# Attention and a routed mixture of experts on one core: the rows of q, k and v loaded in shorter pieces

## Chip, cores and metric

The kernel runs on 1 core of one Trainium2 chip. The metric is the device time of one execution in microseconds. Before the change it is 684.65 us in the median of 3 runs (682.07 to 686.68).

## What is computed

The reference is a causal attention, half of whose heads look at the last 32 positions and half at every 32nd position, followed by a mixture of experts with two levels of routing. Shapes are those of q, k and v: 8 batches, 8 heads, 576 positions, 64 columns, all in float32; 16 experts in 4 groups, of size 512 x 1024 and 1024 x 512.

```python
scores = scale * np.matmul(q, k.transpose(0, 1, 3, 2))          # scale = 1 / 8
rel = pos[:, None] - pos[None, :]
mask_local = (rel >= 0) & (rel < 32)                            # heads 0 to 3
mask_strided = (rel >= 0) & (pos[None, :] % 32 == pos[:, None] % 32)   # heads 4 to 7
attn = softmax(np.where(masks, scores, -1e9)); x = np.matmul(attn, v)
# x as 4608 tokens of 512 columns
g_idx = np.argmax(x @ w_group, axis=1)                          # group, with its softmax weight g_w
e_idx = np.argmax(xg @ w_expert[g], axis=1)                     # expert in it, with weight e_w
out[token] = g_w * e_w * (np.maximum(x[token] @ w1[g, e], 0) @ w2[g, e])
```

## The kernel before

**Layout.** The host rearranges q, k and v into four DRAM tensors: `sq` (q and k of the strided heads, transposed), `ll` (q and k of the local heads, transposed), `vs` and `vl` (v of both, each head with a column of ones). Each has 128 rows a batch, one for each partition. A row is cut into three pieces, one for each group of units: 864, 864 and 648 floats for `sq`, 1024, 1024 and 256 for `ll`, 520, 520 and 390 for `vs`, 520, 520 and 130 for `vl`. In DRAM the pieces of a row start at `SO`, `LO` and `VO`, multiples of 64 floats, and the pitch of a row is a multiple of 64 floats as well. One DMA moves one piece of all 128 rows: one contiguous run a row, up to 4096 bytes.

**Attention.** A batch has five units (`DOUBLES`): two of the strided heads ("s"), two of the local ones ("l") and one of both ("m"). `step(s)` issues the work of four units at once, by hand and in a fixed order on every engine: the QK matmuls of unit s into PSUM (L243, L248), Exp of unit s-1, mask, maximum and subtraction of unit s (DVE L256 and L259, POOL L260), the PV matmuls and the normalization of unit s-2 (L284, L290 to L292), and for unit s-3 the store of x to DRAM (`store_x`, L304 to L313) and its transposes for the routing. POOL copies shifted rows of v (L941, L942).

**Loads.** All loads and stores of this stage are issued by SP, in program order, on one hardware queue. `load_qk` and `load_v` (L916 to L933) load a unit's pieces. Those of the first batch are issued ahead of the loop, with the constants behind the first of them. From then on step g of batch b issues two loads of batch b + 1, behind the stores of that step (`pieces`, L969). Two sets of buffers alternate (`bufs[b % 2]`), so a piece is loaded about one batch before it is read. The first half of expert 0's W1 is loaded within the last batch (L579).

**Instructions.** The attention is written out without loops: the matmuls and weight loads of TensorE in this stage are some 8,700 instructions in a row. Their code comes from DRAM too, in packets of a queue of its own (q8 of the profile) on the same 16 DMA engines.

**Experts.** Behind the attention, tokens are gathered for each expert by indirect DMAs, and two matmuls in three products of split float32 follow (L633, L685). The weights come in pieces of 512 KB: the first weight in rows of 4 KB, the second in rows of two runs of 2 KB (L561).

Of the kernel before, what the change touches and what calls it, by code (L numbers as in the profile page):

```python
# [19 lines left out]
B, H, S, D = 8, 8, 576, 64  # L20
# [26 lines left out]
SW = [8 * 4 * UN // 2, 8 * 4 * UN // 2, 4 * 3 * UN]  # L47
SO = [0, 896, 1792]
SPITCH = 2496
LW = [1024, 1024, 256]  # L50
LO = [0, 1024, 2048]
LPAD = 32
LTILE = LPAD + sum(LW)
VW = 2 * (D + 1)
SVW = [4 * VW, 4 * VW, 3 * VW]
VO = [0, 576, 1152]
SVPITCH = 1600
LVW = [4 * VW, 4 * VW, VW]
LVPITCH = 1344
# [13 lines left out]
CW = SEL0 + G + NE  # L73


def unit_rows(u):

    return min(RES, STRIDE - RES * u)


def unit_order():

    return [t * STRIDE + RES * u + r for u in range(NU) for t in range(TR) for r in range(unit_rows(u))]


def host_arrays(q, k, v, moe_w_group, moe_w_expert, moe_w1, moe_w2):
    f = np.float32
    qT = np.ascontiguousarray(np.asarray(q, f).transpose(0, 1, 3, 2))
    kT = np.ascontiguousarray(np.asarray(k, f).transpose(0, 1, 3, 2))

    byhead = lambda x: x.reshape(B, 2, 2, D, S).transpose(0, 2, 3, 1, 4).reshape(B, 128, 2, S)
    bytoken = lambda x: x.reshape(B, 2, 2, S, D).transpose(0, 2, 3, 1, 4)
    sq = np.zeros((B, 128, SPITCH), f)
    order = unit_order()
    rmaj = lambda x: np.pad(byhead(x[:, 4:])[..., order], ((0, 0), (0, 0), (0, 0), (0, NU * UN - S)))
    both = np.stack([rmaj(qT), rmaj(kT)], axis=2)
    for g in range(3):
        x = both[:, :, :, :, 4 * UN * g:min(4 * g + 4, NU) * UN].reshape(B, 128, -1)
        sq[:, :, SO[g]:SO[g] + SW[g]] = x

    ql = byhead(qT[:, :4])
    kl = byhead(kT[:, :4]).reshape(B, 128, 2, S // 64, 2, 32)[:, :, :, :, ::-1].reshape(B, 128, 2, S)
    both = np.stack([ql, kl], axis=2)
    ll = np.concatenate([both[:, :, :, :, 256 * g:256 * g + 256].reshape(B, 128, -1) for g in range(3)], axis=2)

    v = np.asarray(v, f)
    vs = np.zeros((B, 2, GAP, SVPITCH), f)
    x = np.zeros((B, 2, NU * UN, 2, D + 1), f)
    x[:, :, :S, :, :D] = bytoken(v[:, 4:])[:, :, order]
    x[..., D] = 1.0  # L110
    x = x.reshape(B, 2, NU, UN, VW).swapaxes(2, 3)
    vl = np.zeros((B, 128, LVPITCH), f)
    y = np.ones((B, 2, S, 2, D + 1), f)
    y[..., :D] = bytoken(v[:, :4])
    y = y.reshape(B, 2, S // 64, 2, 32, VW)[:, :, :, ::-1].reshape(B, 2, S // 64, 64, VW)
    y = y.swapaxes(2, 3).reshape(B, 128, S // 64, VW)
    for g in range(3):
        vs[:, :, :UN, VO[g]:VO[g] + SVW[g]] = x[:, :, :, 4 * g:4 * g + 4].reshape(B, 2, UN, -1)
        vl[:, :, VO[g]:VO[g] + LVW[g]] = y[:, :, 4 * g:4 * g + 4].reshape(B, 128, -1)
    wr = np.concatenate([moe_w_group] + [moe_w_expert[g] for g in range(G)], axis=1)  # L120
    wr = np.pad(wr.reshape(4, 128, G + NE).transpose(1, 0, 2), ((0, 0), (0, 0), (0, 32 - G - NE)))

    cst = np.zeros((128, CW), f)
    p = np.arange(128)[:, None]
    w = np.arange(GAP)[None, :]
    i = p % GAP
    for o, m in ((0, RES), (3 * GAP, unit_rows(NU - 1))):
        ok = (w < m * TR) & (i < m * TR) & (w % m == i % m) & (w // m <= i // m)
        cst[:, o:o + GAP] = np.where(ok, 0.0, MASKED)
    key = np.where(p // LB % 2 == 0, w - LB, np.where(w < LB, w, w - 2 * LB))  # L130
    ok = (key <= p % LB) & (key > p % LB - STRIDE)
    cst[:, GAP:2 * GAP] = np.where(ok, 0.0, MASKED)
    cst[:, 2 * GAP:3 * GAP] = np.where(ok & ((key >= 0) | (p >= LB)), 0.0, MASKED)
    cst[:, IOTA0:TRI0] = np.arange(128)
    cst[:, TRI0:SML0] = np.arange(96)[None, :] > p
    sm = cst[:, SML0:WR0]
    cst[:, WR0:SEL0] = wr.reshape(128, -1)
    cst[:, SEL0:] = p % 32 == np.arange(G + NE)
    sm[:, 0:16] = np.arange(16) * (EST // TB)
    sm[:, 16:20] = [4, 3, 2, 1]  # L140
    sm[:, 20:21] = p
    sm[:, 64:64 + NSL] = (EST // 128 * np.arange(NE)[:, None] + np.arange(NB)).reshape(1, -1)
    sm[:, 24:24 + len(NVAR) - 1] = NVAR[:-1]
    sm[:, 48:48 + NTOK // CAP] = CAP * np.arange(1, NTOK // CAP + 1)
    return {
        "sq": sq, "ll": np.ascontiguousarray(ll), "vs": vs.reshape(B, 128, SVPITCH), "vl": vl, "cst": cst,
        "w1": np.ascontiguousarray(moe_w1.reshape(NE, DM, FF)),
        "w2": np.ascontiguousarray(moe_w2.reshape(NE, FF, DM)),
    }
# [148 lines left out]
def store_x(tc, k, b, xd, x, g):  # L298

    nc = tc.nc  # L300
    xb = xd[b * S:(b + 1) * S, :]
    kind, n = DOUBLES[g]
    if kind == "l":
        nc.sync.dma_start(xb[n * 256:(n + 1) * 256, 0:256].rearrange("(u p) c -> p u c", p=128),  # L304
                          x.rearrange("p (u c) -> p u c", c=256))
        return
    xs = xb[:, 256:512].rearrange("(t r) c -> t r c", r=STRIDE)
    for kind, u, a, p in rows_of(g):
        if kind == "s":
            m = unit_rows(u)  # L310
            nc.sync.dma_start(xs[:, RES * u:RES * u + m], x[p:p + m * TR, a * 256:(a + 1) * 256])
    if DOUBLES[g][0] == "m":
        nc.sync.dma_start(xb[512:576, 0:256], x[64:128, 256:512])  # L313
# [490 lines left out]
def build_all(nc, d, out):  # L804
    k = Ctx()
    with tile.TileContext(nc, schedule_with_timeline_sim=True) as tc, ExitStack() as top:
# [86 lines left out]
        with ExitStack() as ms:  # L893
# [6 lines left out]
            for i in range(2):  # L900
                p = early[i].enter_context(pool(f"early{i}", side="right" if i else "left"))
# [7 lines left out]
            def clear(i):  # L909
                _, ll, _, _, even = bufs[i]  # L910
                nc.gpsimd.memset(ll[:, 0:LPAD], 0.0)
                nc.gpsimd.memset(even[:, 0:VW], 0.0)

            clear(0)

            def load_qk(b, g):  # L916
                kind, n = DOUBLES[g]
                sq, ll = bufs[b % 2][:2]
                if kind != "l":
                    nc.sync.dma_start(sq[n], d["sq"][b, :, SO[n]:SO[n] + SW[n]])  # L920
                if kind != "s":
                    nc.sync.dma_start(ll[:, LPAD + LO[n]:LPAD + LO[n] + LW[n]],
                                      d["ll"][b, :, LO[n]:LO[n] + LW[n]])

            def load_v(b, g):
                kind, n = DOUBLES[g]
                _, _, vs, vl, vl2 = bufs[b % 2]
                if kind != "l":
                    nc.sync.dma_start(vs[:, 4 * VW * n:4 * VW * n + SVW[n]],
                                      d["vs"][b, :, VO[n]:VO[n] + SVW[n]])  # L930
                if kind != "s":
                    x, y = 4 * VW * n, 4 * VW * n + LVW[n]
                    nc.sync.dma_start(vl[:, x:y], d["vl"][b, :, VO[n]:VO[n] + LVW[n]])  # L933

            def shift_v(b, g, h):
                n = DOUBLES[g][1]
# [7 lines left out]
            def step(s):  # L944
# [16 lines left out]
                if u:  # L961
                    for g, h in shifts[u.g] if s > 1 else (((1, 0), (1, 64)) if s else ()):
                        shift_v(u.b, g, h)
                    for f in ahead.get(u.g, ()):
                        if u.b + 1 < B:
                            f(u.b + 1)
                run_due()

            pieces = {0: [(load_qk, 0), (load_qk, 1)], 1: [(load_qk, 2), (load_v, 0)],  # L969
                      2: [(load_qk, 3), (load_v, 1)], 3: [(load_qk, 4), (load_v, 2)],  # L970
                      4: [(load_v, 3), (load_v, 4)]}
            ahead = {g: [lambda b, f=f, h=h: f(b, h) for f, h in fs] for g, fs in pieces.items()}
            shifts = [[(1, 0)], [(1, 64)], [(4, 0)], [(4, 64)], [(3, 0), (3, 64)]]
            units = []
            fixed, k.fixed = ExitStack(), True
            fixed.enter_context(tc.manual_schedule())
            load_qk(0, 0)
            load_consts(tc, k, cp, lp, d["cst"])
            load_qk(0, 1)
# [11 lines left out]
            for b in range(B):  # L991
# [5 lines left out]
                for g in range(len(DOUBLES)):  # L997
                    u = Ctx()
# [24 lines left out]
    return k  # L1023


_SHAPES = {"sq": (B, 128, SPITCH), "ll": (B, 128, sum(LW)), "vs": (B, 128, SVPITCH),
           "vl": (B, 128, LVPITCH), "cst": (128, CW),
           "w1": (NE, DM, FF), "w2": (NE, FF, DM)}


def make_program():
    import concourse.bacc as bacc

    nc = bacc.Bacc("TRN2", target_bir_lowering=False, num_devices=1)
    d = {n: nc.dram_tensor(n, s, F32, kind="ExternalInput").ap() for n, s in _SHAPES.items()}
    out = nc.dram_tensor("out", (NTOK, DM), F32, kind="ExternalOutput").ap()
    build_all(nc, d, out)
    return nc
# [8 lines left out]
```

## Time and profile before

| What | Value |
|---|---|
| Median of 3 runs | 684.65 us |
| The profiled execution's own time | 686.05 us |
| Its span in the profile | 684.3 us |
| TensorE busy in the span | 620.5 us (91%) |
| VectorE, ScalarE, GpSimd busy | 394.3, 352.0, 257.7 us |
| DMA packets | 64,120, 127.82 MB |
| Mean granted TensorE clock | 0.966 of full speed |

The profile is of one execution; its span is a little shorter than the time that the device reports. In the slices each digit is a fortieth of the span (17.1 us) in tenths of it; the attention fills about the first eleven. PE is TensorE's matmul, PEld its weight load, DVE VectorE, ACT ScalarE, POOL GpSimd, SP the engine that issues the DMAs; an engine with a q behind it is its sequencer. In a row of waits stand the engine that waited, its line, what ended the wait, the total, the count and the longest; "issue" is time in which the engine waited for nothing that the profile shows. A row of the DMA queues has packets, MB and the time that the packets took as a share of 16 engines over the stretch. A packet is what one engine moves as one piece; each DMA adds a packet of 4 bytes on each of its engines, which are among those under 512 B.

### The profile page before, as it was taken

The numbers are of one execution on the slowest core, as the hardware profiler recorded it, in microseconds if no ns is written. First come the engines' busy times: TensorE is split into PE (matmuls) and PEld (weight loads), VectorE is DVE, ScalarE is ACT, GpSimd is POOL, SyncE is SP. The second block draws the span as 40 slices with busy tenths as digits, with TensorE's granted clock in tenths as the row PEclk, the third lists the DMA queues.
The fourth block names the chain that finished last, engine by engine and source line by source line (L and its number), as shares of the span: only waits on it lengthen the run. The fifth ranks groups of instructions, "written<-read, shape, count | busy, mean of one in ns | idle before, by whom it ended". The sixth has DMA issues, their size and how long they took to land.

```text
span 684.3 us, 17927 instructions
## 1 busy us (share of the span) xinstructions
PE 620.5 (91%) x7140; PEld 530.8 (78%) x7141; DVE 394.3 (58%) x640; ACT 352.0 (51%) x621; POOL 257.7 (38%) x336
## 2 busy tenths in 40 slices
PE   5788778778788999999999999999999999999991
PEld 4666566556547798989989889889898898989981
DVE  6557667667755745575475555774655556455120
ACT  2455536454614645575475555764645557455220
POOL 6558665566623522251332422532324223220110
PEclk9999999999879999999999999999999999999996
DMA  9888876786516663573744936755548465362100
GB/s 334 261 271 248 248 214 188 223 266 196 142 37 203 218 233 126 198 239 131 269 158 149 286 119 236 244 182 198 196 130 274 133 233 184 137 208 82 36 18 23
DMA packets 64120, 127.82 MB, mean 187 GB/s; under 512 B 12640, under 2 KB 24928, under 8 KB 63976
## 3 DMA queue, kind: packets, MB, share of 16 engines
q1 hardware_dynamic: 56296, 106.78, 49.0%
q0 software_dynamic: 7680, 18.91, 7.4%
q8 instruction: 116, 1.90, 1.1%
q14 instruction: 28, 0.23, 0.1%
HBM read 109.91 MB, written 22.04 MB: 193 GB/s over the span
## 4 chain that ended last, share of the span: by engine, by line
PE 66%; issue 3%; DVE 2%; ACT 1%; DMA 1%; POOL 1%; POOLq 0%; DVEq 0%; ACTq 0%
PE pair L633 21%; PE bank L685 16%; PE pair L685 12%; PE bank L633 7%; PE bank L693 4%; PE pair L606 2%; PE pair L847 1%; DMA raw<-w 1%; PE pair L358 1%; DVE wL L565 1%; PE bank L373 0%; POOL out L669 0%; DVE xL L614 0%; ACT wH L564 0%; PE pair L284 0%
## 5 line engine op out<-in xcount | busy, mean ns | idle before, releaser
L565 DVE TENSOR_TENSOR wL<-raw,wH 128x1024 fp32r<-128x1024 f32 x122 | 146.1, 1230 | 29.5 <-ACT wH L564 21.4
L564 ACT CAST wH<-raw 128x1024 fp32r<-128x1024 f32 x124 | 125.7, 1063 | 19.4 <-DMA raw<-w 11.5
L633 PE MATMUL pair<-xH,wH 128*128 128x248 f32 (+10 forms) x384 | 114.0, 297 | 0.6 <-PE bank L847 0.6
L633 PE MATMUL pair<-xL,wH 128*128 128x248 f32 (+10 forms) x384 | 114.1, 297 | 0.0
L633 PE MATMUL pair<-xH,wL 128*128 128x248 f32 (+10 forms) x384 | 114.0, 297 | 0.0
L669 POOL DMA_INDIRECT out<-y,idx x48 | 56.1, 1168 | 143.3 <-ACT y L664 97.7
L652 DVE SCALAR_TENSOR_TENSOR hL<-pair,hH 128x384 fp32r<-128x384 f32 x96 | 53.2, 556 | 86.4 <-ACT hH L651 86.3
L651 ACT ACTIVATE hH<-pair 128x384 fp32r<-128x384 f32 x96 | 47.0, 491 | 96.5 <-PE pair L633 47.9
L633 PEld LDWEIGHTS pair<-xH,wH 128*128 128x128 f32 x384 | 72.3, 188 | 1.8 <-issue 1.1
L633 PEld LDWEIGHTS pair<-xL,wH 128*128 128x128 f32 x384 | 72.3, 188 | 0.6
L633 PEld LDWEIGHTS pair<-xH,wL 128*128 128x128 f32 x384 | 72.2, 188 | 0.0
L656 POOL CAST hX<-hH 128x512 fp32r<-128x512 f32 x16 | 9.8, 611 | 162.8 <-issue 150.2
L594 POOL DMA_INDIRECT xg<-xd,idx x48 | 58.1, 1210 | 18.2 <-issue 14.3
L685 PE MATMUL bank<-wH,hH 128*128 128x512 f32 x160 | 63.4, 396 | 0.0
L685 PE MATMUL bank<-wL,hH 128*128 128x512 f32 x160 | 63.4, 396 | 0.0
L685 PE MATMUL bank<-wH,hL 128*128 128x512 f32 x160 | 63.1, 394 | 0.0
L260 POOL TENSOR_TENSOR pr<-pr,mx 128x512 f32<-128x512 f32 x40 | 41.7, 1041 | 50.5 <-DVE rs L291 27.2
L685 PE MATMUL pair<-wH,hH 128*128 128x512 f32 x128 | 51.8, 405 | 0.7 <-DVE xL L614 0.7
L664 ACT ACTIVATE y<-bank,xg 128x512 f32<-128x512 f32 x32 | 22.0, 688 | 55.8 <-PE bank L685 31.4
L685 PE MATMUL pair<-wH,hL 128*128 128x512 f32 x128 | 50.6, 395 | 0.0
L685 PE MATMUL pair<-wL,hH 128*128 128x512 f32 x128 | 50.5, 394 | 0.0
L614 DVE TENSOR_TENSOR xL<-pair,xH 128x384 fp32r<-128x384 f32 x64 | 33.2, 552 | 25.6 <-ACT xH L613 20.0
(151 smaller groups left out, 1257.1 us busy)
## 6 DMA issues: line engine op xcount, KB each, us to landing
raw<-w SPq DMA_DIRECT2D x124, 512.0 KB
ll<-ll SPq DMA_DIRECT2D x16, 512.0 KB
sq<-sq SPq DMA_DIRECT2D x16, 432.0 KB
xd<-x SPq DMA_DIRECT2D x80, 54.0 KB
vs<-vs SPq DMA_DIRECT2D x16, 260.0 KB
vl<-vl SPq DMA_DIRECT2D x16, 260.0 KB
xd<-x SPq DMA_DIRECT2D x16, 256.0 KB
sq<-sq SPq DMA_DIRECT2D x8, 324.0 KB
```

The costliest lines, as they stand in the source:

```text
L260: nc.gpsimd.tensor_tensor(p3, p3, mx.unsqueeze(2).broadcast_to([128, 8, GAP]), op=ALU.subtract)
L564: nc.scalar.copy(H[:, d], r)
L565: low[j % len(low)].tensor_tensor(L[:, d], r, H[:, d].bitcast(F32), op=ALU.subtract)
L594: self.nc.gpsimd.indirect_dma_start(out=xg, out_offset=None, in_=self.xd, in_offset=bass.IndirectOffsetOnAxis(ap=self.k.idx[:, c:c + 1], a ...
L614: nc.vector.tensor_tensor(self.xL[:, c, :], pt[:, :CAP], self.xH[:, c, :].bitcast(F32), op=ALU.subtract))
L633: self.nc.tensor.matmul(ps[:, :N], a[:, c, cols], x[:, c, :N], start=(n == 0), stop=(n == last))
L651: nc.scalar.activation(self.hH[:, f, :], ps, AF.Relu)
L652: nc.vector.scalar_tensor_tensor(self.hL[:, f, :], ps, 0.0, self.hH[:, f, :].bitcast(F32), ALU.max, ALU.subtract)
L664: nc.scalar.activation(y, ps, AF.Copy, scale=w)
L669: i = nc.gpsimd.indirect_dma_start(out=self.out, out_offset=bass.IndirectOffsetOnAxis(ap=k.idx[:, c:c + 1], axis=0), in_=y, in_offset=None ...
L685: nc.tensor.matmul(ps, a[:, f, s], w[:, f, :], start=(n == 0), stop=(n == 23))
L693: nc.tensor.matmul(ps, self.hX[:, f, :], w[:, f, :], start=(n == 0), stop=(n == 15))
```

## The change

The rows of `sq`, `ll`, `vs` and `vl` are laid out in DRAM in pieces of 130 to 260 floats (520 to 1040 bytes), with 16 floats (64 bytes) between one and the next. A load then takes its piece of a row as two to four runs in place of one, which land side by side in SBUF as before. Two loads keep one run a row: the last of `ll` (1024 bytes) and the last of `vl` (520 bytes). The tiles in SBUF, the order of the loads, their number and their bytes, and all else stay. The pieces' starts are multiples of 64 bytes.

```diff
+SPLIT = {"sq": (SO, SW, [216, 216, 216]), "ll": (LO, LW, [256, 256, 256]),
+         "vs": (VO, SVW, [260, 260, 195]), "vl": (VO, LVW, [260, 260, 130])}
+SPARE = 16
+
+def dram_offsets(name):
+    _, ws, us = SPLIT[name]
+    return np.cumsum([0] + [w // u * (u + SPARE) for w, u in zip(ws, us)]).tolist()
+
+def spread(name, x):
+    out = [np.pad(x[:, :, o:o + w].reshape(B, 128, w // u, u), ((0, 0),) * 3 + ((0, SPARE),)).reshape(B, 128, -1)
+           for o, w, u in zip(*SPLIT[name])]
+    return np.ascontiguousarray(np.concatenate(out, axis=2))
...
+            def fill(tile, b, name, n):
+                o, w, u = (x[n] for x in (dram_offsets(name), *SPLIT[name][1:]))
+                src = d[name][b, :, o:o + w // u * (u + SPARE)].rearrange("p (c u) -> p c u", u=u + SPARE)
+                nc.sync.dma_start(tile.rearrange("p (c u) -> p c u", u=u), src[:, :, 0:u])
...
-                    nc.sync.dma_start(sq[n], d["sq"][b, :, SO[n]:SO[n] + SW[n]])
+                    fill(sq[n], b, "sq", n)
...
-                    nc.sync.dma_start(ll[:, LPAD + LO[n]:LPAD + LO[n] + LW[n]],
-                                      d["ll"][b, :, LO[n]:LO[n] + LW[n]])
+                    fill(ll[:, LPAD + LO[n]:LPAD + LO[n] + LW[n]], b, "ll", n)
...
-                    nc.sync.dma_start(vs[:, 4 * VW * n:4 * VW * n + SVW[n]],
-                                      d["vs"][b, :, VO[n]:VO[n] + SVW[n]])
+                    fill(vs[:, 4 * VW * n:4 * VW * n + SVW[n]], b, "vs", n)
...
-                    nc.sync.dma_start(vl[:, x:y], d["vl"][b, :, VO[n]:VO[n] + LVW[n]])
+                    fill(vl[:, 4 * VW * n:4 * VW * n + LVW[n]], b, "vl", n)
```

## Rows read from the trace of the kernel before

**Rows 1.** The page: span, slices of the DMA engines, packets, the queue of instructions.

```profile
span 684.3 us, 17927 instructions
...
DMA  9888876786516663573744936755548465362100
...
DMA packets 64120, 127.82 MB, mean 187 GB/s; under 512 B 12640, under 2 KB 24928, under 8 KB 63976
...
q8 instruction: 116, 1.90, 1.1%
```

**Rows 2.** Busy time by stretch; the last three columns are clock, DMA share, GB/s.

```profile
60.00:80.00 20.00, 16.04 (x474) 12.34 (x466) 15.19 (x35) 10.49 (x26) 15.75 (x28) 1.00 0.80 239
...
300.00:400.00 100.00, 100.00 (x623) 91.09 (x621) 57.23 (x74) 55.61 (x84) 31.03 (x28) 1.00 0.60 201
```

**Rows 3.** Timeline of TensorE in the first 15 us.

```profile
4.21 1.00 PE L243 MATMUL pair<-sq 64*54 64x54 f32 x32 [4.21 <-DMA sq<-sq]
7.51 1.17 PE L248 MATMUL pair<-ll 64*32 64x64 f32 x64 [2.30 <-DMA ll<-ll]
...
14.21 0.32 PE L248 MATMUL pair<-ll 64*32 64x64 f32 x8 [0.54 <-DMA ll<-ll]
```

**Rows 4.** Waits of TensorE, 0 to 190 us.

```profile
PE pair L284 <- issue: 12.4, 9, 2.8
...
PE pair L243 <- issue: 6.1, 4, 2.4
...
PE pair L248 <- issue: 2.1, 3, 1.1
...
PE bank L358 <- issue: 1.6, 1, 1.6
```

**Rows 5.** Answers by tile (sq, ll, x, raw), 0 to 200 us.

```profile
L243 PE MATMUL pair<-sq x704: 204/210/333, 4.2 to 166.7; 64*54 64x54 f32 x176
...
L922 SPq DMA_DIRECT2D ll<-ll x24: 328/444/1533, 1.7 to 147.0; - x24
...
L304 SPq DMA_DIRECT2D xd<-x x16: 365/380/1337, 21.1 to 184.4; - x16
...
L583 ACT CAST wH<-raw x8: 602/616/623, 174.7 to 183.3; 128x512 fp32r<-128x512 f32 x8
```

**Rows 6.** Busy time in two stretches between stops of TensorE.

```profile
30.40:34.26 3.86, 3.39 (x127) 2.79 (x127) 2.63 (x5) 2.36 (x5) 2.78 (x4) 1.00 0.85 194
34.26:40.01 5.75, 3.41 (x128) 2.41 (x127) 3.20 (x6) 2.73 (x7) 4.13 (x7) 1.00 0.96 321
```

**Rows 7.** Timeline of TensorE at the ends of those stretches.

```profile
34.26 0.24 PE L284 MATMUL pair<-even,pT 64*32 64x65 f32 x2 [0.47 <-issue]
...
40.02 0.69 PE L284 MATMUL pair<-vs,pT 64*64 64x65 f32 x31 [2.18 <-issue]
```

**Rows 8.** DMA queues: 34.90 to 37.57, 37.5 to 37.6, 31.00 to 31.91, 31.9 to 32.0.

```profile
q1 hardware_dynamic: 746, 1.05, 106.1%
...
q8 instruction: 1, 0.02, 71.8%
...
DMA packets 176, 0.18 MB, mean 198 GB/s; under 512 B 37, under 2 KB 167, under 8 KB 175
...
q8 instruction: 1, 0.02, 57.5%
```

**Rows 9.** DMA queues: 62.5 to 63.5, and 3.25 to 4 us.

```profile
q1 hardware_dynamic: 324, 0.36, 102.6%
...
q1 hardware_dynamic: 117, 0.31, 103.6%
```

**Rows 10.** DMA queues, 20 to 150 us.

```profile
q1 hardware_dynamic: 20805, 30.03, 78.2%
```

**Rows 11.** DMA queues, weights of 4 KB (482.8 to 491.4) and 2 KB (494.1 to 504).

```profile
q1 hardware_dynamic: 575, 2.10, 70.2%
...
q1 hardware_dynamic: 1088, 2.10, 69.3%
```

More of the change, by code (lines that the diff above doesn't have):

```diff
@@ L145, in host_arrays @@
     return {
-        "sq": sq, "ll": np.ascontiguousarray(ll), "vs": vs.reshape(B, 128, SVPITCH), "vl": vl, "cst": cst,
+        "sq": spread("sq", sq), "ll": spread("ll", ll), "vs": spread("vs", vs.reshape(B, 128, SVPITCH)),
+        "vl": spread("vl", vl), "cst": cst,
         "w1": np.ascontiguousarray(moe_w1.reshape(NE, DM, FF)),
@@ L928, in load_v @@
                 if kind != "l":
-                    nc.sync.dma_start(vs[:, 4 * VW * n:4 * VW * n + SVW[n]],
-                                      d["vs"][b, :, VO[n]:VO[n] + SVW[n]])
+                    fill(vs[:, 4 * VW * n:4 * VW * n + SVW[n]], b, "vs", n)
                 if kind != "s":
-                    x, y = 4 * VW * n, 4 * VW * n + LVW[n]
-                    nc.sync.dma_start(vl[:, x:y], d["vl"][b, :, VO[n]:VO[n] + LVW[n]])
+                    fill(vl[:, 4 * VW * n:4 * VW * n + LVW[n]], b, "vl", n)
             def shift_v(b, g, h):
@@ L1023, in build_all @@
     return k
-_SHAPES = {"sq": (B, 128, SPITCH), "ll": (B, 128, sum(LW)), "vs": (B, 128, SVPITCH),
-           "vl": (B, 128, LVPITCH), "cst": (128, CW),
+_SHAPES = {**{n: (B, 128, dram_offsets(n)[-1]) for n in SPLIT}, "cst": (128, CW),
            "w1": (NE, DM, FF), "w2": (NE, FF, DM)}
```

## The prediction

> **What bounds the kernel now.** The page comes first: it gives the span, and in the slices of the DMA engines a first stage of some ten (to about 180 us) at six to nine tenths, and a second one that falls and rises [rows 1]. All the loads of q, k and v that the change touches lie in the first. The table of stretches sets TensorE beside it: 16.0 us of 20 busy with the DMA share at 0.80, against 100 of 100 us later [rows 2]. So the second stage is TensorE's own work, no q, k or v load runs in it, and I give it nothing. The question is what holds the first stage.
>
> In the timeline TensorE waits for loads three times, 4.21, 2.30 and 0.54 us, all before 14.3 us, in the first batch [rows 3]. From then on loads come in time, since each is issued a batch before its use. A unit takes 4.28 us (unit 0 starts at 4.2, unit 38 at 166.7 [rows 5]), a batch of five 21.4 us; that is the slack of a load.
>
> The larger item is in the waits of the stage, under "issue": TensorE stands still 17 times for 22.2 us while no semaphore holds it [rows 4]. The stretches between two such stops show what it is. From 30.40 to 34.26 and from 34.26 to 40.01 there are 127 and 128 matmuls, each with its weight load [rows 6]: 256 instructions from stop to stop. The instruction queue moves 1.90 MB in 116 packets [rows 1], 16 KB each, which is 64 bytes for each of 256 instructions. A stop is TensorE waiting for its next block of code. The DMA rows tell why it comes late. In the block entered at 34.26 the instruction packet starts only between 37.5 and 37.6 (71.8% of 1.6 engine-us: it takes 1.15 us), and TensorE goes on at 40.02, a stop of 2.18 us; in the block entered at 30.40 it starts at 31.9 and the stop is 0.47 us [rows 7, 8]. Before the late one, the 16 engines worked through 746 packets, 47 each, at a share of 106%; before the early one 176, 11 each [rows 8]. The code seems to stand behind what is already queued on its DMA engine, mostly q, k, v loads and x stores. The size of that queue, in time, sets the stops.
>
> **The change, part by part.** *Packets.* Per batch and row of 128 partitions, sq goes from 3 packets to 11, ll from 3 to 9, vs from 3 to 6, vl from 3 to 5: 12 to 31, or 1,536 to 3,968 packets, 152 more for each engine. Bytes, instructions, semaphores and order stay. Two stretches with few stalls price a packet: 324 packets, 0.36 MB in 1.0 us at 102.6% are 50.7 ns for 1,111 B; 117 packets, 0.31 MB in 0.75 us at 103.6% are 106 ns for 2,650 B [rows 9]. The line through both is 36 ns per 1,000 B and 10.6 ns per packet. So 152 x 10.6 ns = 1.6 us of DMA time a batch. The DMA does 78.2% x 21.4 = 16.7 us a batch now [rows 10]: plus 9.6%, to a share near 0.86. The weights bound this: expert halves of 2.10 MB come in 575 packets of 4 KB or 1,088 of 2 KB, 32 more an engine, and take 6.04 against 6.86 us [rows 11], which is 26 ns per packet more. The other end is nothing: shorter packets may also lose less in the stalls that longer ones had; below it there is little room, as the bytes stay. Range 0 to 26 ns, so 0 to 4.0 us a batch; I take 10.6, since those packets are nearest in size. In the steady state nothing waits for it: every load has 21.4 us.
>
> [...]
>
> *Start.* Here the loads are waited for. sq and ll of unit 0 and 1 carry 24 extra packets per engine each: 48 x 10.6 ns = 0.5 us more at the wait of 7.51. Up to the ll piece waited for at 14.21, nine loads carry 136: 1.4 us. Between 0.5 and 1.4 us; I take +1.0.
>
> *Issue on SP.* A load now has up to four runs a row. The x store of two runs a row takes 380 ns to issue, an ll load 444 ns in the median (328 at least, the store 365) [rows 5]: 0 to 0.15 us more a load, up to 1.8 us of SP a batch. What covers it is the batch that a load has until its use. Behind a load on SP stand the stores of x; their tiles are seven deep, so that a store may come some units late before a new x waits for its tile. If that cover went, up to 1.8 us a batch would move.
>
> *The code's wait.* The queue ahead of it was 2.7 us in the late case. Two ends. If the queue holds the same work, it is 9.6% longer: 0.26 us x 17 stops = +4.4 us. If it holds a limited count of packets, it is shorter: 47 packets of the new mean (3.73 MB / 3,968 = 939 B, 44.5 ns) are 2.1 us in place of 2.67, 0.6 us x 17 = -10. No row shows which of the two the queue holds, and none is nearer to one end, so I take the middle, -3. Not all of a shorter stop arrives at the end: behind it DVE (15 of 20 us busy) is next late [rows 2].
>
> *Weights and end of stage.* The last ll load is issued at 147.0, the first expert's raw loads come behind it, and their first cast starts at 174.7 [rows 5]: 1.6 us more queue is covered there by far.
>
> Sum against the profiled execution's 686.05 us (span 684.3, 1.75 around it; 1.4 above the median of 684.65): +1.0 start, 0 steady loads, 0 SP, -3 code = -2.0. On the median: 682.5.
>
> **Rivals.** *A, the code comes clearly sooner.* The queue ahead of it is a count of packets, and small ones pass faster: -10 + 1.0 = -9, 675.5. For: the stops follow the packets ahead (47 against 11). Against: in the same rows the time ahead differs as much.
>
> *B, the queue grows.* An extra packet costs what the weights show, 26 ns: 4.0 us a batch on 16.7, the share to 0.97 and the queue 24% longer: 0.65 us x 17 = 11, less what other waits absorb, plus 1.0 at the start: 695. It lies in the code's wait, in front of QK and PV matmuls, and it decides from about 20 ns per packet on. For: the share is at 0.8 already [rows 2], so little slack is left. Against: packets of about the new size cost 10.6 ns more each, not 26 [rows 9].
>
> *C, the code does not queue behind loads,* or the pieces reach the engines joined as before: nothing but the start moves, 684.65 to 685.7. [...] The 47 packets that went ahead here do not agree.
>
> **Numbers.** About 1% (7 us) is what a measurement can tell from no change. Chances: the forecast 0.43, A 0.26, B 0.20, C 0.11. A lies beyond 1% below; B beyond 1% above; the forecast and C are within. Some of A's mass ends within 1% and some of the forecast's outside it, evenly enough: faster 0.26, same 0.54, slower 0.20. The likeliest case alone spans 678 to 688 (code -8 to +4, start +0.5 to +1.4). The range goes on to A and B, leaving out what lies beyond both: 673 to 695.
>
> **What would show it.** Right: 64,120 + 8 x 2,432 = some 83,600 DMA packets in all; first waits for sq and ll at 4.2 and near 8 us; "issue" stops of TensorE near 19 us in place of 22.2; the stage's DMA share 0.82 to 0.90. A shows in "issue" below 13 us; B in "issue" over 30 us and in waits for loads after 20 us. Wrong would be a change of TensorE's busy time in the second stage, or long waits of TensorE for sq or ll in steady batches: then small reads themselves, not the code behind them, set the pace.

## The result, and the profile after

The changed kernel takes 689.34 us in the median of 16 runs (685.87 to 695.33); the kernel before, timed beside it, 685.79 (682.07 to 689.27, 16 runs). The ratio is **1.0062 [1.0035, 1.0090]**: some 4 us slower, where the forecast was 2 us faster. The time lies inside the forecast range and inside the 1% that the forecast called no change; the direction is wrong, and the interval excludes it. The ratios of the experiments leave out four runs of the kernel before (692.74, 693.34, 1,164.35 and 1,993.36 us) and differ from the quotients of the medians given beside them by up to 0.002.

The page of the profile after, the lines that answer to [rows 1]:

```profile
span 685.9 us, 17927 instructions
...
DMA  9888796895416763663844837655647465362100
DMA packets 83576, 127.82 MB, mean 186 GB/s; under 512 B 12640, under 2 KB 53600, under 8 KB 83432
```

The packets are the forecast ones, at the same bytes and instructions. The profiled execution took 687.63 us, 1.6 more than that of before, and is itself 1.7 below its median; so its trace shows less than half of the loss, and single rows are read here with the other kernels' beside them.

Busy time by stretch, as in [rows 2]:

```profile
60.00:80.00 20.00, 15.70 (x534) 12.76 (x531) 13.40 (x31) 10.86 (x28) 14.41 (x25) 1.00 0.82 231
300.00:400.00 100.00, 100.00 (x615) 90.86 (x614) 58.28 (x75) 56.02 (x84) 32.71 (x29) 1.00 0.61 205
```

Answers by line and tile: the loads of ll on SP, the last matmuls of the attention, and the first and last gather of the second stage (0 to 200 us, the last one the whole span):

```profile
L938 SPq DMA_DIRECT2D ll<-ll x24: 368/476/1645, 1.8 to 146.1; - x24
...
L303 PE MATMUL pair<-vl,pT x576: 213/217/315, 15.3 to 180.6; 64*32 64x65 f32 x192
...
L613 POOL DMA_INDIRECT xg<-xd,idx x48: 994/1016/1975, 202.2 to 584.5; - x48
```

Before:

```profile
L284 PE MATMUL pair<-vl,pT x576: 213/217/313, 14.8 to 179.2; 64*32 64x65 f32 x192
...
L594 POOL DMA_INDIRECT xg<-xd,idx x48: 994/1016/2064, 201.0 to 582.9; - x48
```

So the first stage ends 1.4 us later, the first gather starts 1.2 us later, and from the first gather to the last it is 382.3 us against 381.9. In this trace the loss is in the stage with the loads; the kernels below bear that out. An ll load takes 476 ns to issue in place of 444 [rows 5].

The start, as in [rows 3] (start, us busy, engine, line, operation, and in brackets the idle time before it):

```profile
4.27 1.00 PE L262 MATMUL pair<-sq 64*54 64x54 f32 x32 [4.27 <-DMA sq<-sq]
7.91 1.17 PE L267 MATMUL pair<-ll 64*32 64x64 f32 x64 [2.63 <-DMA ll<-ll]
...
14.67 0.32 PE L267 MATMUL pair<-ll 64*32 64x64 f32 x8 [0.72 <-DMA ll<-ll]
```

Against 7.51 and 14.21 that is 0.40 and 0.46 us later.

Waits of TensorE, 0 to 195 us, as in [rows 4]:

```profile
PE pair L303 <- issue: 13.6, 9, 2.8
PE pair L262 <- issue: 5.6, 2, 3.0
PE pair L262 <- DMA sq<-sq: 4.3, 1, 4.3
PE pair L267 <- issue: 3.4, 3, 1.9
PE pair L267 <- DMA ll<-ll: 3.4, 2, 2.6
...
PE bank L377 <- issue: 0.4, 1, 0.4
```

The stops for code are 15, of 23.0 us in all. Before, with one of 0.3 us that [rows 4] leave out, they were 18, of 22.5: in this profile the sum did not fall. No wait for sq or ll is added to those of the first batch.

The longest stop shows what stands ahead of the code. The matmuls are the same in both kernels, so the same block can be set beside it in the kernel before. Timeline of TensorE at both ends of the block, and the DMA queues in it, from 0.6 us behind its entry until the code packet starts, then the next 0.1 us; first of before (148.8 to 152.1, 152.1 to 152.2):

```profile
148.18 0.77 PE L248 MATMUL pair<-ll 64*32 64x64 f32 x54 [0.56 <-issue]
...
154.48 0.31 PE L243 MATMUL pair<-sq 64*54 64x54 f32 x6 [2.40 <-issue]
```

```profile
q1 hardware_dynamic: 576, 1.03, 93.1%
...
q8 instruction: 1, 0.02, 64.0%
```

Then of after (148.1 to 151.8, 151.8 to 151.9):

```profile
147.47 0.77 PE L267 MATMUL pair<-ll 64*32 64x64 f32 x54 [0.50 <-issue]
...
154.33 0.34 PE L262 MATMUL pair<-sq 64*54 64x54 f32 x3 [2.96 <-issue]
```

```profile
q1 hardware_dynamic: 1200, 1.11, 99.4%
...
q8 instruction: 1, 0.02, 63.8%
```

After, the engines move nothing but 1,200 data packets, 75 each, in 3.7 us; only then does the packet of code start. Before it was 576, 36 each, in 3.3 us. So twice as many packets go ahead of the code, with 8% more bytes, in 12% more time: the wait goes with the work that is queued and not with a count of packets.

Busy time of TensorE (matmuls, weight loads), the other engines, granted clock, DMA share and GB/s in the stage; first of before, then of after:

```profile
20.00:170.00 150.00, 120.30 (x3706) 94.74 (x3706) 99.88 (x217) 78.40 (x193) 92.92 (x149) 0.94 0.79 235
```

```profile
20.00:170.00 150.00, 122.19 (x3691) 96.72 (x3692) 98.37 (x216) 76.78 (x189) 92.75 (x149) 0.90 0.82 237
```

About as many matmuls take 1.9 us longer, at a granted clock of 0.90 in place of 0.94. That is one profile of each: the clock of this stretch differs between profiles of kernels with the same steady loads too, as the trials show. What a lower clock costs can be read behind the longest stop, where the same 66 or 67 matmuls follow up to the next 64 of ll; first of before, then of after:

```profile
154.48:158.25 3.77, 3.59 (x66) 3.00 (x66) 3.27 (x8) 1.25 (x3) 1.75 (x3) 1.00 1.05 367
```

```profile
154.33:160.28 5.95, 5.95 (x67) 5.17 (x67) 4.28 (x9) 1.71 (x4) 3.36 (x4) 0.50 0.97 335
```

After, the granted clock is 0.50 of full speed here in place of 1.00, and the same work takes 5.95 us in place of 3.77: 37% of the time at the lower clock is lost.

Last the DMA queue of the steady batches, 20 to 150 us, as in [rows 10]:

```profile
q1 hardware_dynamic: 36371, 30.65, 82.4%
```

The window holds 30.65 MB against 30.03, so the shares are compared per MB: 82.4% of 130 us over 30.65 MB is 3.50 us per MB, before 3.39. That measure, DMA time per MB, goes with every experiment below. In the four kernels whose steady loads are whole rows (before, start_only, whole_off, ballast) it lies between 3.36 and 3.42.

### The profile page after: what moved, and what is told of

The parts are those of the page before. It is cut to its first block, busy times and chain, and to the rows that moved or that the text cites. A ratio compares the mean times of both kernels' runs of the same rounds, so it can differ in the third digit from the quotient of the medians.

```text
span 685.9 us, 17927 instructions
## 1 busy us (share of the span) xinstructions
PE 622.9 (91%) x7140; PEld 533.4 (78%) x7141; DVE 393.4 (57%) x640; ACT 351.9 (51%) x621; POOL 258.2 (38%) x336
## 2 busy tenths in 40 slices
DMA packets 83576, 127.82 MB, mean 186 GB/s; under 512 B 12640, under 2 KB 53600, under 8 KB 83432
## 4 chain that ended last, share of the span: by engine, by line
PE 67%; issue 3%; DVE 2%; ACT 1%; DMA 1%; POOL 1%; POOLq 0%; ACTq 0%; DVEq 0%
PE pair L652 21%; PE bank L704 16%; PE pair L704 12%; PE bank L652 7%; PE bank L712 4%; PE pair L625 2%; PE pair L866 1%; DMA raw<-w 1%; PE pair L377 1%; DVE wL L584 1%; PE pair L303 0%; PE bank L392 0%; ACT wH L583 0%; PE bank L353 0%; POOL out L688 0%
## 5 line engine op out<-in xcount | busy, mean ns | idle before, releaser
L584 DVE TENSOR_TENSOR wL<-raw,wH 128x1024 fp32r<-128x1024 f32 x122 | 146.1, 1230 | 29.8 <-ACT wH L583 26.9
L704 PE MATMUL bank<-wL,hH 128*128 128x512 f32 x160 | 63.5, 397 | 0.0
```

The lines of the kernel that those rows point to most:

```text
L584: low[j % len(low)].tensor_tensor(L[:, d], r, H[:, d].bitcast(F32), op=ALU.subtract)
L704: nc.tensor.matmul(ps, a[:, f, s], w[:, f, :], start=(n == 0), stop=(n == 23))
```

## The experiments

Two theories stood at the outset. **DMA time** (the queue theory of the expectations)**:** the small packets make the stage's DMA time longer, and the code behind them waits longer. **Alignment:** most new pieces start off a 256-byte boundary in DRAM, and that is the cost; in the kernel before no load of q, k or v starts off one, so this was a supposition that its trace could not show. Beside them, that it is **the start** alone. Ratios are to the kernel before, timed on the same chip. Each run gave one profile; the changed kernel, run twice, has two.

**after2: the changed kernel again.** No edit.

> The changed kernel once more, beside the three that follow, for a second profile of it. Every theory: 1.003 to 1.009 of the time before, 2 to 6 us more. In its profile the queue theory (extra packets lengthen the work that stands ahead of TensorE's code in the steady batches) wants stops of TensorE under issue of 24 us or more, against 22.5 us in the kernel before; the start theory (only the first batch's loads land later) wants them unchanged and the 17th block of code reached as much later as the second.

Measured: 1.0035 [1.0008, 1.0061], 688.05 against 685.88 us. The loss repeats, at 2 to 4 us. The sign in the profile does not: the stops for code sum to 20.1 us, where the theory of DMA time wanted 24 or more and the kernel before had 22.5. Two profiles of one kernel thus differ by 2.9 us in this sum.

```profile
PE pair L303 <- issue: 9.6, 7, 3.0
PE pair L262 <- issue: 4.8, 2, 2.4
PE pair L267 <- issue: 2.4, 2, 1.8
PE bank L377 <- issue: 1.9, 1, 1.9
PE bank L287 <- issue: 1.4, 1, 1.4
```

**start_only and steady_only: one part of the change each.** The pieces are kept for batch 0 alone, or for batches 1 to 7 alone; the other batches read whole rows from the old layout.

```
 def fill(tile, b, name, n):
+    if not (b == 0):        # start_only;  steady_only: if not (b > 0)
+        o, w = SPLIT[name][0][n], SPLIT[name][1][n]
+        nc.sync.dma_start(tile, d[name + "_w"][b, :, o:o + w])
+        return
...
```

> Only batch 0 is loaded in short pieces, batches 1 to 7 in whole rows as before. Start theory: the whole loss is here, ratio 1.004 to 1.007 (3 to 4 us). Queue theory: only the later landing of the first loads is left, +0.5 us, ratio 1.000 to 1.002. Alignment theory (pieces off the 256-byte boundary are dearer): as the queue theory, 1.000 to 1.002.

> Batch 0 in whole rows as before, batches 1 to 7 in short pieces. Queue theory: nearly all of the loss, ratio 1.004 to 1.006 (+3 to +4 us), first wait for ll at 7.5 us as before. Start theory: ratio 0.999 to 1.001.

Measured: start_only 1.0012 [0.998, 1.0045], steady_only **1.0033 [1.0011, 1.0055]**, 688.21 us. Start of TensorE in start_only:

```profile
4.20 1.00 PE L263 MATMUL pair<-sq 64*54 64x54 f32 x32 [4.20 <-DMA sq<-sq]
7.83 1.17 PE L268 MATMUL pair<-ll 64*32 64x64 f32 x64 [2.63 <-DMA ll<-ll]
...
14.52 0.44 PE L268 MATMUL pair<-ll 64*32 64x64 f32 x8 [0.49 <-DMA ll<-ll]
```

The start pays 0.3 us here, too little for the time to tell from none. The steady batches, in which no load is waited for, carry most: 2.3 us, at 1.0033 just under the 1.004 to 1.006 that the theory of DMA time gave. Their DMA queue, 20 to 150 us:

```profile
q1 hardware_dynamic: 35464, 29.76, 80.6%
```

3.52 us per MB. The start alone is ruled out as the cause.

**whole_off and aligned: boundaries without packets, packets without boundaries.** whole_off keeps one run a row and sets the runs 64 bytes apart, so that nine in ten start off a 256-byte boundary; aligned keeps the pieces and starts each on a 256-byte boundary.

```
 whole_off
-SPLIT = {"sq": (SO, SW, [216, 216, 216]), "ll": (LO, LW, [256, 256, 256]), ...
+SPLIT = {"sq": (SO, SW, [864, 864, 648]), "ll": (LO, LW, [1024, 1024, 256]), ...
 aligned
-SPARE = 16
+def pitch(u):
+    return -(-(u + 1) // 64) * 64
...
-    return np.cumsum([0] + [w // u * (u + SPARE) for w, u in zip(ws, us)]).tolist()
+    return np.cumsum([0] + [w // u * pitch(u) for w, u in zip(ws, us)]).tolist()
...
```

> One run a row as before, but the pieces of a row 64 bytes apart, so that most runs start off a 256-byte boundary; packets as before (64,120). Alignment theory: it keeps most of the loss, ratio 1.003 to 1.006. Queue theory by packets, and start theory: nothing, 0.998 to 1.002.

> Pieces and packets of the changed kernel (83,576), but every run starts on a 256-byte boundary (gaps of 160 to 256 bytes). Alignment theory: the loss goes, ratio 0.999 to 1.002. Queue theory by packets: the loss stays, ratio 1.003 to 1.006.

Measured: whole_off 1.0008 [0.9976, 1.0039], aligned **1.0065 [1.003, 1.010]**. The DMA queue, 20 to 150 us, of whole_off and of aligned:

```profile
q1 hardware_dynamic: 20822, 30.14, 79.2%
```

```profile
q1 hardware_dynamic: 35693, 29.98, 80.2%
```

3.42 and 3.48 us per MB. Runs off the boundary cost nothing that shows; aligned pieces cost as much as the others, at 1.0065 even a little more than the 1.003 to 1.006 that the theory of DMA time gave. The alignment theory falls. Between the pieces off the boundary (3.50) and those on it (3.48) there is 0.02 us per MB; a batch moves 30.03 MB x 21.4 / 130 = 4.94 MB, so that is 0.1 us a batch.

**fine: more packets.** Pieces of 432 to 520 bytes, 113,273 packets.

```
-SPLIT = {"sq": (SO, SW, [216, 216, 216]), "ll": (LO, LW, [256, 256, 256]), ...
+SPLIT = {"sq": (SO, SW, [108, 108, 108]), "ll": (LO, LW, [128, 128, 128]), ...
```

> Pieces of 432 to 520 bytes: 61 packets a row and batch in place of 31, 3,840 more a batch, so some 2.0 us more DMA time a batch again (8 to 9 ns each). Queue theory (DMA time per packet, in the steady batches): DMA time from 24 to 150 us near 115 us in place of 103.7, and a loss two to four times that of the change: ratio 1.010 to 1.025. Clock theory (short packets change when TensorE stops, and the granted clock falls more often, with no tie to the DMA time): ratio as the change's, 1.003 to 1.008.

Measured: **1.0131 [1.0074, 1.0189]**, 694.36 against 686.61 us. DMA queue, 20 to 150 us, and the third wait of the start:

```profile
q1 hardware_dynamic: 56796, 29.06, 88.8%
```

```profile
16.29 0.44 PE L267 MATMUL pair<-ll 64*32 64x64 f32 x8 [3.02 <-DMA ll<-ll]
```

3.97 us per MB; the start loses 2.1 us (16.29 against 14.21), the rest of the kernel some 6. The ratio lies in the 1.010 to 1.025 of the theory of DMA time; its interval only touches the 1.003 to 1.008 of the clock theory, by which the clock falls more often without a tie to the DMA time. The loss grows with the DMA time, but not in proportion: the rise in us per MB is five times that of the change.

**ballast: DMA time without small packets.** The kernel before, with two extra loads of 1,728-byte rows during each of batches 1 to 6 into a tile that the attention stage leaves unused; 1,728 packets more.

```
+def ballast(b, g):
+    if b < B - 1:
+        r = raw_p.tile([128, 1024], F32, name="raw")
+        nc.sync.dma_start(r[:, 0:432], d["sq"][b, :, SO[g]:SO[g] + 432])
...
+pieces[0].append((ballast, 0))
+pieces[2].append((ballast, 1))
```

> The kernel before, with two more loads for each of batches 1 to 6, of 1728 bytes a row into tiles that nothing reads: 16 packets more on each engine a batch, 1.15 us of DMA time, about what the change's packets add (1.0 us), with 256 packets a batch in place of 2,432. Queue theory by time: the same loss as the change's steady part, ratio 1.002 to 1.006. A theory by which the number of packets does it, not their time: 0.999 to 1.001.

Measured: **1.0046 [1.0011, 1.0082]**, 688.93 us. DMA queue, 20 to 150 us, and busy time, 20 to 170:

```profile
q1 hardware_dynamic: 22288, 32.00, 82.6%
```

```profile
20.00:170.00 150.00, 121.61 (x3613) 95.88 (x3616) 98.07 (x213) 76.68 (x189) 92.68 (x148) 0.90 0.83 250
```

The stage's DMA time is 107.4 us of 130 in place of 101.7: 5.7 more, where the change adds 0.11 x 30.03 = 3.3 at the same bytes. The us per MB are as before (3.36). So more DMA time, with hardly more packets and nothing waiting for the extra loads, does damage of the same size; by a theory of the number of packets the ratio would have been 0.999 to 1.001.

**no_loads: the other direction.** The kernel before without the loads of batches 2 to 7 (the attention of those batches runs on the data of the first two). Only the attention stage is read; the second stage, which gathers by what the first computed, is another one here.

```
-    if u.b + 1 < B:
+    if u.b + 1 < 2:
```

> The kernel before without the loads of batches 2 to 7, which compute again on what batches 0 and 1 left; the routing and so the experts' part differ, so only the attention stage is to be read (some 185 us before). If TensorE's stops under issue are code that stands behind loads: they go from 22 us to under 5, the code packets start 0.5 to 1.3 us after the block is entered in place of 2.3 on average, and the stage is 12 to 22 us shorter. If code is late for another reason: stops as before, the stage within 4 us.

TensorE's stops, 0 to 160 us; the last matmuls of the stage; the DMA queue, 20 to 150; busy time, 20 to 140:

```profile
PE pair L284 <- issue: 4.6, 7, 1.4
...
PE pair L248 <- issue: 1.3, 1, 1.3
...
PE pair L243 <- issue: 0.9, 1, 0.9
...
PE bank L334 <- issue: 0.2, 1, 0.2
```

```profile
L284 PE MATMUL pair<-vl,pT x576: 213/217/312, 14.8 to 156.6; 64*32 64x65 f32 x192
```

```profile
q1 hardware_dynamic: 14554, 12.57, 33.7%
```

```profile
20.00:140.00 120.00, 107.09 (x3505) 84.70 (x3506) 94.56 (x205) 72.86 (x181) 88.69 (x142) 0.99 0.36 101
```

The stage ends 22.6 us sooner (156.6 against 179.2), though before no steady load was ever waited for. The stops for code in the whole stage are 7.0 us in place of 22.5: not the "under 5" that was expected, but 15.5 us less; the stage is shortened by a little more than the 12 to 22 us expected. The clock is 0.99 (0.94 before, over the same stretch). How soon behind the entry of its block a code packet starts there is not shown. By the stops the loads do hold up the code, and with it TensorE.

**What the trials settle.** By ratio and DMA time the kernels fall into two groups: whole rows in the steady batches without ballast (before, start_only, whole_off), at 1.000 to 1.001, and everything with more DMA time (after, after2, steady_only, aligned, ballast, fine), at 1.003 to 1.013, though the intervals of the smaller ones overlap with those of the first. The stage with the loads agrees: its last matmul (the L303 row of the result section) starts at 179.2, 180.0 and 180.7 us in the profiles of before, start_only and whole_off, and at 180.6, 181.9, 182.2, 183.7, 182.9 and 186.3 in after, after2, steady_only, aligned, ballast and fine: means of 180.0 and 182.9.

How the extra DMA time reaches TensorE is settled only in part. The stops sum, in the same order, to 22.5, 19.9 and 21.7 us, and to 23.0, 20.1, 24.2, 24.6, 24.5 and 26.9: means of 21.4 and 23.9, with overlap. The clock of the stretch from 20 to 170 us is 0.94, 0.92 and 0.91 in the first group, and 0.90, 0.89, 0.89, 0.89, 0.90 and 0.92 in the second. Start_only and whole_off lose no time that shows, so much of the fall from 0.94 to 0.90 in the result section can be chance; and fine, which loses most, is not low. Busy time of whole_off and of fine:

```profile
20.00:170.00 150.00, 120.53 (x3691) 95.28 (x3691) 98.06 (x216) 77.06 (x189) 92.61 (x148) 0.91 0.80 234
```

```profile
20.00:170.00 150.00, 118.05 (x3631) 92.78 (x3629) 97.87 (x211) 76.35 (x188) 92.03 (x147) 0.92 0.92 236
```

The granted clock over the whole program, of the timed runs that have it on record, is 0.9603 in the mean of the first group (78 runs) and 0.9580 of the second (70 runs): 0.0023 lower, give or take 0.0019. In the traces of before and after each of the 16 recorded spells of the clock is at 1.00 or at 0.50. Between these two levels, 0.0023 is 0.46% of 686 us more at 0.50, 3.2 us; at the 37% lost behind the longest stop that is about 1.2 us, an estimate from one stretch. Longer stops and a lower clock could so share the 2 to 4 us; profiles that differ by 2.9 us between two runs of one kernel can't divide it. No version beat both kernels. No second profile of the kernel before was taken, and setting the two loads of a step apart, so that fewer packets stand back to back ahead of a code packet, was not tried on the chip.

## Why the prediction was wrong, point by point

**The code's wait** is the step that failed: "If it holds a limited count of packets, it is shorter", -10, weighed evenly against the same work taking longer, +4.4, and -3 taken between them. The queue does not hold a count: in the same block 75 packets an engine went ahead in 3.7 us where 36 had in 3.3, with 8% more bytes. The stops did not get shorter: their sum, 22.5 us before, is 23.0 and 20.1 in the two profiles of the changed kernel; over the four profiles with these pieces in the steady batches it is 23.0 in the mean against 21.4 in the three of the first group, where the forecast was 3 less. By time the kernel is 2 to 4 us slower. So the end at -10 should have had no weight, and rival A with its 0.26 neither. That could have been argued ahead of the result: a load is a fixed number of bytes, issued at a fixed step, and what stands in the queue is loads; cutting their rows finer cuts no load out.

**The price of a packet** was sized three times too high. Forecast: 1.6 us of DMA time a batch on 16.7, from two stretches of 1.0 and 0.75 us [rows 9]. Measured: per MB 3.50 (after), 3.49 (after2, from 30.07 MB at 80.8%), 3.52 and 3.48 against 3.39, so +0.11; at 4.94 MB a batch that is 0.54 us a batch, 3.6 ns for each of 152 packets. Down to half the size, in fine, it is 0.58 x 4.94 = 2.9 us for 384 packets, 7.6 ns each; the step from the pieces to the half ones alone is 2.4 us for 232 packets, 10 ns each. So one price for every packet does not hold over these sizes.

**"In the steady state nothing waits for it: every load has 21.4 us", 0,** holds for the loads themselves: no wait for sq or ll is new after the first batch. But the stage still pays for the longer DMA time, as steady_only and ballast show. The forecast did have that path, through the code; it had it with the wrong sign in the middle.

**Start,** +1.0 between 0.5 and 1.4: measured 0.40 and 0.46 us, just below the lower end. With 3.6 ns in place of 10.6, 136 packets are 0.49 us.

**Issue on SP,** 0: right. 476 against 444 ns for ll, 467 against 462 for sq; no store of x was late enough to be waited for.

**Weights and second stage,** 0: right; 382.3 against 381.9 us from first gather to last.

**The rivals.** B has the mechanism, the queue grows with the work in it, at a far smaller price: 3.6 ns a packet and not 26. Its point of decision, 20 ns, was wrong with it: that was where the loss would outweigh a gain, and there was no gain. The even-handed end of the code's wait, +4.4, with the start, 690 us, was the nearest thing to the truth, and for the wrong size of each part: a third of the DMA time, and a larger effect for each us of it. C is refuted by no_loads: with the loads gone, two thirds of the stop time goes; in the block of the longest stop of after 75 packets of data an engine went ahead of the code; and the pieces do not reach the engines joined, with 83,576 packets.

**Slips in the working.** 684.65 - 2.0 is 682.65 and not 682.5. With code from -8 to +4 and the start from +0.5 to +1.4 the likeliest case spans 677 to 690 and not 678 to 688; the measured 689.34 lies at its end. And the pieces do not start at multiples of 64 bytes, as was said ahead of the prediction: the gap is 64 bytes, but 864 + 64 bytes are 14.5 times 64, and 1,040 + 64 are 17.25 times. Some half of the starts are at multiples of 64, one in eight at multiples of 256. That changes nothing here, as the boundary made no difference that shows.

## What to carry to other kernels

In this kernel, where TensorE's code comes in over the same DMA engines as the data (q8 at 1.3% of the 16 engines' time beside q1 at 78.2%, 20 to 150 us before), a DMA that nobody waits for was not free: at a DMA share of 0.8, 3 to 6 us of extra DMA time in 130 us of the stage cost 2 to 4 us of the kernel, as small packets or as more bytes. Ask of any change to transfers how many us of DMA time it adds or removes, and look for the queue ahead of the code to follow that time and not the count of packets: in the block set side by side twice as many packets, with 8% more bytes, took 12% more time. Taking DMA time out of a stage with stops under "issue" is worth trying even when every load already arrives early: here the stage ended 22.6 us sooner without three quarters of its loads.

## What the runs showed of the hardware

Cutting rows of 1,560 to 4,096 bytes into pieces of 780 to 1,040 cost 3.6 ns of DMA time for each added packet in this traffic, and down to 432 to 520 bytes 7.6 ns. Whether runs in DRAM start on a 256-byte boundary or off one made no difference that 12 to 16 runs of each show (whole rows off it: 1.0008 [0.9976, 1.0039]; pieces on it 1.0065 [1.003, 1.010], off it 1.0035 and 1.0062).

Removing three quarters of the loads shortened an attention stage that never waited for them by 22.6 us of 179, of which 15.5 us are fewer and shorter stops for code. The clock was 0.99 in place of 0.94 over 20 to 140 us; how much of the other 7.1 us that is was not measured.
